# Decode kernel: other cuts of the loads, 1728 floats of kept V in three PSUM banks, 3840 floats of the first W_q held, first MLP in 22 loads

## The chip, the core and the metric

The kernel runs on one core of a Trainium2 chip. TensorE (PE) multiplies, VectorE (DVE) and ScalarE (ACT) work on rows, SyncE (SP) issues nearly all loads. The loads are carried by 16 DMA engines from HBM into SBUF. The metric is the device time of one execution in microseconds (us); three runs were taken of the kernel before.

## The reference

One token for each of four sequences goes through attention and a gated MLP, twice, with the same weights and caches in both layers. Only the last 1024 of 4096 cached positions are used. All data are float32.

```python
x = A_x                                            # 4 x 1 x 640
x = x + _A_ref(_layernorm(x), k_cache, v_cache, wq, wo)
x = x + _B_ref(_layernorm(x), W_gate, W_up, W_down)
x = x + _A_ref(_layernorm(x), k_cache, v_cache, wq, wo)
x = x + _B_ref(_layernorm(x), W_gate, W_up, W_down)
# _A_ref: q = x @ wq (32 heads of 128); softmax(q k^T / sqrt(128)) v over 1024 positions; then @ wo
# _B_ref: h = relu(x @ W_gate) * (x @ W_up), 1728 wide; h @ W_down
```

## The kernel before

Everything the kernel multiplies by lies in HBM as three matrices of 128 rows: `heads` (W_q, K, V, W_o of 27 heads, in the order of use), `kept` (the same of the last five heads, 27 to 31) and `mlp` (25,920 columns: the products of the last 192 hidden units first, then three gates of 5120 columns, then W_down in blocks of 640). A column is one float32 in each of 128 partitions, 512 bytes; sizes below are in columns, which the code and the title call floats.

In SBUF there is one large tile `store` of 51,840 columns, and `first_q` with the first 3072 columns of `heads`, which stay for both layers. At the end of layer 0's attention the 47,360 columns of `kept` lie at the start of `store` (`FRONT` is their end) and are used again at the start of layer 1, without a second load. All else is loaded twice.

The list of loads, `plan`, is written out by hand in the order in which SP issues them: layer, matrix, first and last column, place in `store`. `live` marks the columns of `store` that are still in use. After each product, `done` marks its operand's columns free, and `load` issues loads from the list for as long as the next one's place is free. SP then waits for the product that frees the place. So the order of issue is fixed, and a load can hold up those behind it.

Groups of heads are worked on in turn: the scores of the next group (line 396, PE), its softmax (line 407, ACT), then the values of this group (line 427, PE) and the projection of the one before (line 461). Layer 0 runs groups 0 to 8, with the kept groups 7 and 8 last (`K0`, `K1`); layer 1 begins with these two.

Between the two attentions stands the first MLP. Its weights don't fit beside `kept`, so they go through a ring of six places: three of 1280 columns behind `FRONT`, the last 640 columns of `store`, and two places taken from `kept`. `AHEAD` is 768 columns of the kept W_q; line 484 copies them into `probs`. `BACK` is 1280 columns of the kept V of head 29; line 485 copies 1024 of them into the two PSUM banks of `ps`, and line 435 copies 256 into the right part of `po`. In layer 1, when the K below `HOME` has been used, lines 400 and 401 copy the V from PSUM into `store` at `HOME`. `get` finds the place of an operand: in `first_q`, in `probs`, at `HOME`, or in the load that has it. It wants the whole operand in one place, so loads end where products end. Two products are cut in two by hand, at `CUT` (line 363) and at the start of `BACK` (line 426).

In `forward`, `gate(3)` uses the first 1920 columns, `gate(0)` to `gate(2)` 5120 each in products of 256 columns (line 519, four at a time on four parts of the array), and `down` W_down in blocks of 640 as four products of 160 (line 550), with a filler product (line 298) behind each block in layer 0.

The ring of the first MLP and the loads behind it:

```python
slots = [FRONT, FRONT + 1280, FRONT + 2560, BACK[0], AHEAD[0], STORE - D]
for i, n in enumerate([1280] * 4 + [768, 512] + [(768, 512), 1280, 1280, 1280, 768, 512]
                      + [1280, 1280, 1280, WD0 + D + 2 * QUARTER - 17280, D, D] + [1280] * 4 + [D, D]):
```

Of the kernel before, what the change touches and what calls it, by code (L numbers as in the profile page):

```python
# [59 lines left out]
HELD = 3072  # L60
STORE = 51840
# [4 lines left out]
BACK = FRONT - 2 * KV - 1280, FRONT - 2 * KV  # L66
HOME = 12672
# [22 lines left out]
CUT = 1792  # L90
ROWS["heads"][2].append(len(HEADS[0]) * D + CUT)
ROWS["heads"][2].sort()
ROWS["mlp"] = {}, MLP, [*range(0, GU0, P), *range(GU0, WD0, 256), WD0, TAIL, *range(WD1, MLP + 1, D)]
# [5 lines left out]
def decode_kernel(ctx: ExitStack, tc: tile.TileContext, x, source, sel, out):  # L99
# [20 lines left out]
    def put(layer, row, to, *cuts):  # L120

        for lo, hi in zip(cuts, cuts[1:]):
            assert hi - lo <= MOST and to % 64 == 0 and lo in known[row] and hi in known[row], (row, lo, hi)
            assert to + hi - lo <= STORE, (row, lo, hi, to)
            plan.append((layer, row, lo, hi, to))
            to += hi - lo
        return to
# [18 lines left out]
    known = {row: set(cuts) for row, (_, _, cuts) in ROWS.items()}  # L146
# [23 lines left out]
    assert lo == MLP  # L170


    k, cut = at_part("k", 0), at_part("q", 1) + CUT
# [7 lines left out]
    lo, to = lo + 8704, HOME + BACK[1] - BACK[0]  # L181
    for n in 4608, 6144, 9728:
        hi = near(lo + n)
        to = put(1, "heads", to, lo, hi)
        lo = hi
# [34 lines left out]
    def get(layer, row, lo, n):  # L220
        if row == "heads" and lo + n <= HELD:
            return first_q[:, lo:lo + n]
        if row == "kept" and layer and AHEAD[0] <= lo < AHEAD[1]:
            return probs[:, QUARTER + lo - AHEAD[0]:][:, :n]
        if row == "kept" and layer and BACK[0] <= lo < BACK[1]:
            return store[:, HOME + lo - BACK[0]:][:, :n]
        for first, m, p in held[key(layer, row)]:
            if first <= lo and lo + n <= first + m:
                return store[:, p + lo - first:p + lo - first + n]
        raise KeyError((layer, row, lo, n))  # L230
# [18 lines left out]
    def part(layer, what, h, lo, n):  # L249

        row, first = WHERE[what, h]
        return get(layer, row, first + lo, n)
# [26 lines left out]
    nc.vector.memset(pp, 0.0)  # L279
# [8 lines left out]
    y = ps_y.tile([P, QUARTER], F32, name="y")  # L288
# [68 lines left out]
    def query(layer, g, spread=False):  # L357


        n = len(HEADS[g]) * P  # L360
        qp[g] = ps_m.tile([P, n], F32, tag="m", name="qp")
        for c in range(KC - 1):
            for a, b in [(0, CUT - c * n), (CUT - c * n, n)] if g == 1 and c * n < CUT < c * n + n else [(0, n)]:
                nc.tensor.matmul(qp[g][32 * c:32 * c + 32, a:b], xT[:, B * c:B * c + 32],  # L364
                                 part(layer, "q", g, c * n + a, b - a),
                                 start=True, stop=c > 0 and not spread or b < n, tile_position=(0, 32 * c))
        part_done(layer, "q", g, 0, (KC - 1) * n)
        c = KC - 1
        m = n // 4 if spread else n
        for a in range(n // m):  # L370
            nc.tensor.matmul(qp[g][32 * a:32 * a + 32, a * m:a * m + m], xT[:, B * c:B * c + 32],  # L371
                             part(layer, "q", g, c * n + a * m, m), start=False, stop=True, tile_position=(0, 32 * a))
        part_done(layer, "q", g, c * n, n)
# [14 lines left out]
    def scores(layer, g):  # L388
        n = len(HEADS[g])
        to = sc[g] = pp if layer and g == order[1][0] else ps  # L390
        for i, h in enumerate(HEADS[g]):
            for j in range(2):
                for b in range(B):
                    lo = (j * B + b) * 512
                    at = SIDE - 1 + SIDE * (B * i + b) - i
                    nc.tensor.matmul(to[32 * b:32 * b + SIDE, j, :], qT[:, at:at + SIDE], part(layer, "k", h, lo, 512),  # L396
                                     start=i == 0, stop=i == n - 1, tile_position=(0, 32 * b))
                    part_done(layer, "k", h, lo, 512)
                    if to is pp and k0 + i * KV + lo < HOME + BACK[1] - BACK[0] <= k0 + i * KV + lo + 512:
                        nc.scalar.copy(store[:, HOME:HOME + 1024], ps.rearrange("p j n -> p (j n)"))  # L400
                        nc.scalar.copy(store[:, HOME + 1024:HOME + 1280], po[:, P:3 * P])
        nm[g] = small.tile([P, 1], F32, name="nm")
        nc.vector.tensor_reduce(nm[g], to.rearrange("p j n -> p (j n)"), axis=AX.X, op=ALU.max, negate=True)  # L403
# [9 lines left out]
    def values(layer, g, last=False):  # L413


        n = len(HEADS[g])
        for i, h in enumerate(HEADS[g]):
            t = pT[i % 2]
            to = t[:, GAP:].rearrange("p (c x) -> p c x", c=8)[:, :, :B]
            for j in range(2):  # L420
                nc.vector.tensor_copy(to[:, 4 * j:4 * j + 4], pp[:, j].rearrange("p (c x) -> p c x", c=4)[:, :, i:P:32])  # L421
            for c in range(8):
                a = c % 4
                at = GAP + SIDE * B * c - B * i
                cut = BACK[0] - at_part("v", h) - c * 512
                for x, z in [(0, cut), (cut, 512)] if g >= K0 and 0 < cut < 512 else [(0, 512)]:
                    nc.tensor.matmul(po[32 * a:32 * a + SIDE * B, x:z], t[:, at:at + SIDE * B],  # L427
                                     part(layer, "v", h, c * 512 + x, z - x),
                                     start=i == 0 and c < 4, stop=i == n - 1 and c >= 4 and z == 512, tile_position=(0, 32 * a))
                part_done(layer, "v", h, c * 512, 512)  # L430
        if last:
            nc.vector.tensor_copy(gates[:, 2 * P:], po[:, 2 * P:])  # L432
            nc.scalar.copy(gates[:, :2 * P], po[:, :2 * P])
            if layer == 0:
                nc.scalar.copy(po[:, P:3 * P], store[:, BACK[1] - 256:BACK[1]])
                free(*BACK)
        else:
            nc.scalar.copy(gates, po)  # L438
# [18 lines left out]
    def project(layer, g, last=False):  # L457
        o = oT.pop(g)
        for i, h in enumerate(HEADS[g]):
            for a in range(4):  # L460
                nc.tensor.matmul(y[32 * a:32 * a + B], o[:, i], part(layer, "o", h, a * QUARTER, QUARTER),  # L461
                                 start=False, stop=last and h == HEADS[g][-1], tile_position=(0, 32 * a))
            part_done(layer, "o", h, 0, D)

    def attention(layer):
# [14 lines left out]
        for before, g, after, then in zip([None] + gs, gs, gs[1:] + [None], gs[2:] + [None] * 2):  # L480
            totals(g)
            turned()
            if layer == 0 and after is None:
                nc.scalar.copy(probs[:, QUARTER:QUARTER + 768], store[:, AHEAD[0]:AHEAD[1]])
                nc.scalar.copy(ps.rearrange("p j n -> p (j n)"), store[:, BACK[0]:BACK[0] + 1024])
                free(*AHEAD)
# [21 lines left out]
    def forward(layer):  # L508
# [3 lines left out]
        def gate(j):  # L512
# [3 lines left out]
            for c in range(KC):  # L516
                for g in range(groups):
                    lo = at + (c * groups + g) * 2 * n
                    nc.tensor.matmul(gus[j][32 * g:32 * g + 32, :2 * n], xT[:, B * c:B * c + 32], get(layer, "mlp", lo, 2 * n),  # L519
                                     start=c == 0, stop=c == KC - 1, tile_position=(0, 32 * g))  # L520
# [24 lines left out]
        def down(j, last=False):  # L545
            for f in range(4 if j < 3 else 1):
                lo = WD1 + j * WD + f * D if j < 3 else WD0
                w = get(layer, "mlp", lo, D)
                for g in range(4):
                    nc.tensor.matmul(y[32 * g:32 * g + B], hTs[j][:, f], w[:, g * QUARTER:(g + 1) * QUARTER],  # L550
                                     start=False, stop=last and f == 3, tile_position=(0, 32 * g))
# [5 lines left out]
            if j == 3:  # L557
                w = get(layer, "mlp", TAIL, 2 * QUARTER)
                for g in range(4):
                    r = slice(64 * (g // 2), 64 * (g // 2) + 64)  # L560
                    nc.tensor.matmul(y[32 * g:32 * g + B], hTs[j][r, 1], w[r, g % 2 * QUARTER:(g % 2 + 1) * QUARTER],
                                     start=False, stop=False, tile_position=(r.start, 32 * g))
# [83 lines left out]
```

## Time and profile before

| | |
|---|---|
| median of three runs | 733.49 us (733.29 to 733.76) |
| profiled execution | 733.02 us |
| its span, first to last instruction | 731.2 us |
| read from HBM | 311.19 MB, 426 GB/s over the span |
| mean granted TensorE clock | 0.818 |
| loads issued by SP: `heads`, `kept`, `mlp` | 46 with that of `first_q`, 10, 34 |

A row of the windows view has, for one stretch of the span, the busy time of each engine and its number of instructions, the granted clock, the mean busy share of the 16 DMA engines and the rate. A row of the landing times has the time from a load's issue to the semaphore that says it is in. A row of the chain of waits has start, length and what ran or was waited for. A timeline row has start, length, engine, line, operation, tiles and count, and in brackets the idle time before it with what ended it. One product in float32 is two matmul records in the trace.

### The profile page before, as it was taken

How to read it: one execution, taken by the hardware profiler on the slowest of the kernel's cores; microseconds unless marked ns; L12 is line 12 of the kernel's file. 1: busy time of each engine (PE TensorE's matmuls, PEld its weight loads, DVE VectorE, ACT ScalarE, POOL GpSimd, SP SyncE). 2: the span in 40 equal slices, each digit the busy share in tenths (PEclk: the TensorE clock that was granted, in tenths of full speed). 3: DMA queues.
4: the chain of work that ended last, by engine and by line, in shares of the span. 5: the costliest groups of instructions: out<-in, count | busy, mean ns of one | idle time of the engine just before them, and what ended most of it. 6: DMA issues, size and time to landing. Idle time of an engine off the chain costs nothing.

```text
span 731.2 us, 8241 instructions
## 1 busy us (share of the span) xinstructions
PE 440.8 (60%) x3755; PEld 140.9 (19%) x3755; DVE 76.1 (10%) x280; ACT 50.5 (7%) x93; POOL 0.2 (0%) x4
## 2 busy tenths in 40 slices
PE   0846565655555555519778995465656556555576
PEld 0211111111111111103333231021111012111233
DVE  1111000010010101002101221001011010101011
ACT  0200000000000000000301210000000000000100
POOL 0000000000000000000000000000000000000000
PEclk9978787877777787759999999677778677877999
DMA  9999999999999999999999999999999999999996
GB/s 414 400 445 438 445 438 405 439 444 438 422 430 438 422 443 442 422 428 421 421 401 410 437 426 452 427 445 425 442 438 411 445 440 444 410 435 432 428 425 286
DMA packets 13290, 311.80 MB, mean 426 GB/s; under 512 B 1476, under 2 KB 1732, under 8 KB 6984
## 3 DMA queue, kind: packets, MB, share of 16 engines
q1 hardware_dynamic: 13104, 311.19, 99.1%
q8 instruction: 29, 0.48, 0.2%
q10 hardware_dynamic: 152, 0.09, 0.0%
q14 instruction: 5, 0.04, 0.0%
HBM read 311.19 MB, written 0.08 MB: 426 GB/s over the span
## 4 chain that ended last, share of the span: by engine, by line
DMA 75%; PE 23%; DVE 1%; issue 1%; ACT 0%; SPq 0%; ACTq 0%; DVEq 0%
DMA store<-in_heads 56%; PE ps L396 9%; DMA store<-in_kept 9%; DMA store<-in_mlp 7%; PE po L427 5%; DMA sel_sb<-in_sel 3%; PE qp L364 1%; PE pp L411 1%; PE y L461 1%; PE qp L371 1%; PE pp L396 1%; PE pp L519 1%; PE qt L383 1%; PE ot L451 0%; PE y L550 0%
## 5 line engine op out<-in xcount | busy, mean ns | idle before, releaser
L396 PE MATMUL ps<-store,qT 128*4 128x512 f32 x976 | 154.1, 711 | 119.9 <-DMA store<-in_heads 97.9
L427 PE MATMUL po<-store,pT 128*16 128x512 f32 (+1 forms) x1028 | 151.9, 708 | 122.4 <-DMA store<-in_heads 116.5
L427 PEld LDWEIGHTS po<-store,pT 128*16 128x16 f32 x1028 | 32.5, 109 | 226.9 <-issue 118.5
L396 PEld LDWEIGHTS ps<-store,qT 128*4 128x4 f32 x976 | 28.4, 95 | 227.3 <-DMA store<-in_heads 110.0
L403 DVE TENSOR_REDUCE nm<-ps 128x1 f32<-128x1024 f32 x17 | 20.8, 1225 | 255.4 <-PE ps L396 255.4
L407 ACT ACTIVATE probs<-ps,nm 128x1024 f32<-128x1024 f32 x17 | 18.9, 1113 | 328.8 <-DVE nm L403 328.8
L421 DVE COPY pT<-pp 128x16 f32<-128x16 f32 x128 | 17.1, 169 | 135.1 <-PE po L427 135.1
L461 PE MATMUL y<-store,oT 128*4 128x160 f32 x512 | 23.6, 317 | 10.6 <-DMA store<-in_heads 9.0
L438 ACT COPY gates<-po 128x512 f32<-128x512 f32 x16 | 9.4, 586 | 247.6 <-PE po L427 247.6
L519 PE MATMUL pp<-store,xT 128*32 128x256 f32 (+1 forms) x300 | 21.8, 363 | 6.7 <-DVE gates L529 3.1
L411 PE MATMUL pp<-sel_sb,probs 128*128 128x128 f32 x144 | 20.8, 293 | 0.0
L411 PEld LDWEIGHTS pp<-sel_sb,probs 128*128 128x128 f32 x144 | 18.7, 155 | 0.0
L364 PE MATMUL qp<-store,xT 128*32 128x512 f32 (+2 forms) x124 | 18.5, 586 | 0.0
L444 DVE RECIPROCAL r<-so 128x16 f32<-128x16 f32 x18 | 4.6, 257 | 131.2 <-PE so L442 131.2
L461 PEld LDWEIGHTS y<-store,oT 128*4 128x4 f32 x512 | 12.8, 90 | 19.6 <-DMA store<-in_heads 9.4
L371 PE MATMUL qp<-store,xT 128*32 128x512 f32 (+3 forms) x38 | 15.1, 505 | 0.0
L376 DVE TENSOR_SCALAR gates<-qp,rstd 128x512 f32<-128x512 f32 (+2 forms) x18 | 12.4, 690 | 17.5 <-PE qp L371 16.0
L291 PE MATMUL y<-probs,sel_sb 4*4 4x160 f32 x8 | 0.7, 444 | 21.2 <-DMA sel_sb<-in_sel 21.2
L519 PEld LDWEIGHTS pp<-store,xT 128*32 128x32 f32 x300 | 10.0, 109 | 16.3 <-DMA store<-in_mlp 7.1
L550 PE MATMUL y<-store,hT 128*4 128x160 f32 x208 | 10.3, 299 | 3.5 <-DMA store<-in_mlp 3.4
L383 PE MATMUL qt<-sel_sb,gates 128*128 128x128 f32 x64 | 12.3, 315 | 0.0
L451 PE MATMUL ot<-sel_sb,gates 128*128 128x128 f32 x72 | 11.3, 277 | 1.2 <-DVE gates L432 1.2
(79 smaller groups left out, 133.2 us busy)
## 6 DMA issues: line engine op xcount, KB each, us to landing
store<-in_heads SPq DMA_DIRECT2D x20, 7936.0 KB, 45.2
store<-in_heads SPq DMA_DIRECT2D x3, 8128.0 KB, 36.0
store<-in_mlp SPq DMA_DIRECT2D x15, 640.0 KB, 6.6
store<-in_kept SPq DMA_DIRECT2D x2, 4096.0 KB, 40.7
store<-in_heads SPq DMA_DIRECT2D x1, 8000.0 KB, 43.7
store<-in_heads SPq DMA_DIRECT2D x1, 7744.0 KB, 46.0
store<-in_heads SPq DMA_DIRECT2D x1, 7552.0 KB, 35.8
store<-in_heads SPq DMA_DIRECT2D x1, 7424.0 KB, 34.6
```

Of the source, the lines that this page charges most:

```text
L364: nc.tensor.matmul(qp[g][32 * c:32 * c + 32, a:b], xT[:, B * c:B * c + 32], part(layer, "q", g, c * n + a, b - a), start=True, stop=c > 0 ...
L371: nc.tensor.matmul(qp[g][32 * a:32 * a + 32, a * m:a * m + m], xT[:, B * c:B * c + 32], part(layer, "q", g, c * n + a * m, m), start=False ...
L376: nc.vector.tensor_scalar(gates[:, :len(HEADS[g]) * P], qp.pop(g), rstd, SCALE, op0=ALU.mult, op1=ALU.mult)
L383: nc.tensor.transpose(qt[:, i], gates[:, i * P:(i + 1) * P], ident)
L396: nc.tensor.matmul(to[32 * b:32 * b + SIDE, j, :], qT[:, at:at + SIDE], part(layer, "k", h, lo, 512), start=i == 0, stop=i == n - 1, tile_ ...
L403: nc.vector.tensor_reduce(nm[g], to.rearrange("p j n -> p (j n)"), axis=AX.X, op=ALU.max, negate=True)
L407: nc.scalar.activation(probs, sc.pop(g).rearrange("p j n -> p (j n)"), AF.Exp, bias=nm.pop(g), accum_out=sums[g])
L411: nc.tensor.transpose(pp[:, c // 4, c % 4 * P:c % 4 * P + P], probs[:, c * P:(c + 1) * P], ident)
L421: nc.vector.tensor_copy(to[:, 4 * j:4 * j + 4], pp[:, j].rearrange("p (c x) -> p c x", c=4)[:, :, i:P:32])
L427: nc.tensor.matmul(po[32 * a:32 * a + SIDE * B, x:z], t[:, at:at + SIDE * B], part(layer, "v", h, c * 512 + x, z - x), start=i == 0 and c ...
L461: nc.tensor.matmul(y[32 * a:32 * a + B], o[:, i], part(layer, "o", h, a * QUARTER, QUARTER), start=False, stop=last and h == HEADS[g][-1], ...
L519: nc.tensor.matmul(gus[j][32 * g:32 * g + 32, :2 * n], xT[:, B * c:B * c + 32], get(layer, "mlp", lo, 2 * n), start=c == 0, stop=c == KC - ...
```

## The change

- `first_q` holds 3840 columns and `store` has 51,072, so layer 1's loads of `heads` begin at column 3840.
- `BACK` is 1728 columns. 1024 of them rest in `ps`, 384 in `po` and 320 in the bank of `y`, whose tile `yy` is now 512 columns wide with the accumulator `y` in its first 160. `HOME` moves with it.
- The first MLP goes through five places of 1280, 1792, 768, 1728 and 640 columns in the same order throughout, 22 loads in all with one of 640 first and one of 448 last; before, 26.
- The first loads of layer 1 are 2624, 768, 1728, 640 and 448 columns into these places, from column 3840 on in order, then 1216, 1024, 1024, 2048 and 3584 into the place of the kept W_q and K.
- `get` is replaced by `place` and `product`: an operand that lies in two loads is multiplied in two pieces. Loads may end at any multiple of 64 columns.
- The memset of `pp` at the start is gone.

```diff
-HELD = 3072
-STORE = 51840
+HELD = 3840
+STORE = 51072
-BACK = FRONT - 2 * KV - 1280, FRONT - 2 * KV
-HOME = 12672
+BACK = FRONT - 2 * KV - 1728, FRONT - 2 * KV
+HOME = 12864
...
-    slots = [FRONT, FRONT + 1280, FRONT + 2560, BACK[0], AHEAD[0], STORE - D]
     lo = put(0, "mlp", STORE - D, 0, D) - STORE + D
-    for i, n in enumerate([1280] * 4 + [768, 512] + [(768, 512), 1280, 1280, 1280, 768, 512]
-                          + [1280, 1280, 1280, WD0 + D + 2 * QUARTER - 17280, D, D] + [1280] * 4 + [D, D]):
-        for m in n if type(n) is tuple else [n]:
-            put(0, "mlp", slots[i % 6] if m == n or m == 768 else FRONT + 768, lo, lo + m)
-            lo += m
+    slots = [(FRONT, 1280), (FRONT + 1280, STORE - D - FRONT - 1280), (AHEAD[0], 768), (BACK[0], 1728), (STORE - D, D)]
+    for i in range(21):
+        at, n = slots[i % 5]
+        end = min(lo + n, MLP)
+        put(0, "mlp", at, lo, end)
+        lo = end
+    rest = (MLP - D) % (STORE - FRONT + 768 + 1728)
...
-    to = put(1, "heads", FRONT, k, k + 1536, k + 2560, k + 3584)
-    put(1, "heads", BACK[0], HELD, cut)
-    put(1, "heads", AHEAD[0], cut, k)
-    put(1, "heads", to, k + 3584, k + 4096)
-    lo = k + 4096
-    to = put(1, "heads", AHEAD[1], lo, lo + 1024, lo + 2048, lo + 3072, lo + 5120, lo + 8704)
+    lo = HELD
+    for at, n in (FRONT + rest, STORE - D - FRONT - rest), *slots[2:], (FRONT, rest):
+        put(1, "heads", at, lo, lo + n)
+        lo += n
+    to = AHEAD[1]
+    for n in 1216, 1024, 1024, 2048, 3584:
+        to = put(1, "heads", to, lo, lo + n)
+        lo += n
-    for n in 4608, 6144, 9728:
+    for n in 4096, 6144, 9728:
...
+    def place(layer, row, lo):
+        if row == "heads" and lo < HELD:
+            return first_q, lo, HELD - lo
+        most = KV
+        if row == "kept" and layer:
+            if AHEAD[0] <= lo < AHEAD[1]:
+                return probs, QUARTER + lo - AHEAD[0], AHEAD[1] - lo
+            if BACK[0] <= lo < BACK[1]:
+                return store, HOME + lo - BACK[0], BACK[1] - lo
+            most = min(x - lo for x in (AHEAD[0], BACK[0], FRONT) if x > lo)
+        for first, m, p in held[key(layer, row)]:
+            if first <= lo < first + m:
+                return store, p + lo - first, min(first + m - lo, most)
+
+    def product(out, by, layer, row, lo, n, start, stop, rows=slice(0, P), **how):
+        a = 0
+        while a < n:
+            t, p, m = place(layer, row, lo + a)
+            z = min(n, a + m)
+            nc.tensor.matmul(out[:, a:z], by, t[rows, p:p + z - a], start=start and not a, stop=stop and z == n, **how)
+            a = z
...
-    y = ps_y.tile([P, QUARTER], F32, name="y")
+    yy = ps_y.tile([P, 512], F32, name="y")
+    y = yy[:, :QUARTER]
...
-                        nc.scalar.copy(store[:, HOME + 1024:HOME + 1280], po[:, P:3 * P])
+                        nc.scalar.copy(store[:, HOME + 1024:HOME + 1408], po[:, P:])
+                        nc.scalar.copy(store[:, HOME + 1408:HOME + 1728], yy[:, QUARTER:3 * QUARTER])
...
-                nc.scalar.copy(po[:, P:3 * P], store[:, BACK[1] - 256:BACK[1]])
+                nc.scalar.copy(po[:, P:], store[:, BACK[0] + 1024:BACK[0] + 1408])
...
                 nc.scalar.copy(ps.rearrange("p j n -> p (j n)"), store[:, BACK[0]:BACK[0] + 1024])
+                nc.scalar.copy(yy[:, QUARTER:3 * QUARTER], store[:, BACK[1] - 320:BACK[1]])
```

More of the change, by code (lines that the diff above doesn't have):

```diff
@@ L218, in key @@
         return (0 if row == "kept" else layer), row
[L220 to L226, printed above, removed]
-        for first, m, p in held[key(layer, row)]:
-            if first <= lo and lo + n <= first + m:
-                return store[:, p + lo - first:p + lo - first + n]
-        raise KeyError((layer, row, lo, n))
+    def place(layer, row, lo):
[8 more added lines that the diff above has]
+            most = min(x - lo for x in (AHEAD[0], BACK[0], FRONT) if x > lo)
+        for first, m, p in held[key(layer, row)]:
+            if first <= lo < first + m:
+                return store, p + lo - first, min(first + m - lo, most)
+        raise KeyError((layer, row, lo))
+    def product(out, by, layer, row, lo, n, start, stop, rows=slice(0, P), **how):
[5 more added lines that the diff above has]
+            a = z
     def done(layer, row, lo, n):
@@ L251, in part @@
         row, first = WHERE[what, h]
-        return get(layer, row, first + lo, n)
+        return layer, row, first + lo, n
     def part_done(layer, what, h, lo, n):
@@ L362, in query @@
         for c in range(KC - 1):
[L363 to L366, printed above, removed]
+            product(qp[g][32 * c:32 * c + 32], xT[:, B * c:B * c + 32], *part(layer, "q", g, c * n, n),
+                    start=True, stop=c > 0 and not spread, tile_position=(0, 32 * c))
         part_done(layer, "q", g, 0, (KC - 1) * n)
@@ L424, in values @@
                 at = GAP + SIDE * B * c - B * i
[L425 to L429, printed above, removed]
+                product(po[32 * a:32 * a + SIDE * B], t[:, at:at + SIDE * B], *part(layer, "v", h, c * 512, 512),
+                        start=i == 0 and c < 4, stop=i == n - 1 and c >= 4, tile_position=(0, 32 * a))
                 part_done(layer, "v", h, c * 512, 512)
@@ L460, in project @@
             for a in range(4):
-                nc.tensor.matmul(y[32 * a:32 * a + B], o[:, i], part(layer, "o", h, a * QUARTER, QUARTER),
-                                 start=False, stop=last and h == HEADS[g][-1], tile_position=(0, 32 * a))
+                product(y[32 * a:32 * a + B], o[:, i], *part(layer, "o", h, a * QUARTER, QUARTER),
+                        start=False, stop=last and h == HEADS[g][-1], tile_position=(0, 32 * a))
             part_done(layer, "o", h, 0, D)
@@ L547, in down @@
                 lo = WD1 + j * WD + f * D if j < 3 else WD0
[L548 removed]
                 for g in range(4):
[L550 to L551 removed]
+                    product(y[32 * g:32 * g + B], hTs[j][:, f], layer, "mlp", lo + g * QUARTER, QUARTER,
+                            start=False, stop=last and f == 3, tile_position=(0, 32 * g))
                 done(layer, "mlp", lo, D)
```

31 lines of the change are left out of this document (11 added, 20 removed).

## The prediction

> **What bounds the kernel now.** I read the page first (busy shares, transfer rows, chain), then the windows view over stages, then landing times of the loads that SP issues, and last TensorE's timeline in the first MLP.
>
> ```profile
> span 731.2 us, 8241 instructions
> PE 440.8 (60%) x3755; PEld 140.9 (19%) x3755; DVE 76.1 (10%) x280; ACT 50.5 (7%) x93; POOL 0.2 (0%) x4
> DMA  9999999999999999999999999999999999999996
> q1 hardware_dynamic: 13104, 311.19, 99.1%
> q8 instruction: 29, 0.48, 0.2%
> DMA 75%; PE 23%; DVE 1%; issue 1%; ACT 0%; SPq 0%; ACTq 0%; DVEq 0%
> ```
>
> The DMA engines are busy in every slice but the last; the loads alone fill 99.1% of 16 engines' span. The chain names PE for 23%, but those are stretches in which PE was working while transfers ran as well: it can follow one path only. So the time is bytes over rate, plus what the engines idle.
>
> ```profile
> 480.00:690.00 210.00, 124.20 (x935) 36.99 (x937) 18.88 (x75) 11.02 (x18) 0.00 (x0) 0.77 1.00 434
> 371.00:373.00 2.00, 1.97 (x20) 0.56 (x18) 0.00 (x0) 0.00 (x0) 0.00 (x0) 1.00 0.96 316
> 373.00:395.00 22.00, 17.50 (x201) 7.18 (x203) 1.58 (x7) 1.10 (x3) 0.00 (x0) 1.00 1.03 415
> 363.00:395.00 32.00, 25.84 (x334) 11.75 (x328) 2.89 (x13) 2.39 (x8) 0.00 (x0) 1.00 1.02 406
> 395.00:450.00 55.00, 52.50 (x506) 18.13 (x501) 12.93 (x40) 9.75 (x18) 0.00 (x0) 1.00 1.02 434
> 690.00:727.00 37.00, 26.05 (x392) 11.89 (x388) 4.10 (x17) 2.77 (x9) 0.00 (x0) 0.95 0.93 398
> ```
>
> Columns: stretch, length, busy time of PE, PEld, DVE, ACT, POOL, granted clock, DMA share, GB/s. Large loads run at 434 GB/s. The first MLP (363 to 395) gets 406: its 26 loads are small, and between 371 and 373 the rate falls to 316 with a share of 0.96, the one place in the middle of the run where the engines run short. The last 37 us show something else:
>
> ```profile
> 696.96 30.70 DMA store<-in_mlp
> ```
>
> This link of the chain is the last load: issued at 696.96, landed 30.7 us later, so from 697 on the queue holds all that is left, and still the share of 690 to 727 is 0.93. The 16 engines don't finish together; the end waits for the latest of them.
>
> ```profile
> DMA to landing us min/median/max: 13.5/43.8/62.4
> DMA to landing us min/median/max: 5.1/5.6/8.9
> DMA to landing us min/median/max: 5.6/6.7/7.3
> DMA to landing us min/median/max: 30.7/39.6/49.1
> out_x<-probs SPq DMA_DIRECT2D x1, 80.0 KB, 1.6
> ```
>
> The first four rows are the loads of line 211, by issue: 0 to 340, 363 to 372, 372 to 391, 447 to 690. Loads of the heads wait behind 30 us of queue and more (13.5 is the least, ahead of the first MLP); nothing a few microseconds long can empty that. In the first MLP a load lands 5 to 7 us after its issue, and a 640 KB load moves in 1.5 us (655,360 B at 434 GB/s), so 4 to 5 us is queue and start. The last row is a transfer into an empty queue: 1.6 us, 0.2 of it for its bytes, so a load needs at most 1.4 us from issue to landing beside its bytes. A load issued with less than that queued ahead can leave engines idle.
>
> **The change, part by part.**
>
> *768 more floats of W_q stay.* Layer 1 starts its reload at column 3840 and not 3072: 768 x 512 B = 393,216 B less, 0.91 us at 434 GB/s (0.92 at the mean 426). Layer 0 moves the same bytes. As transfers fill the span, all of it is on the path: **-0.91**. The first load is longer by as much, but the loads behind it take 43.8 us to land at the median, so nothing early in layer 0 reaches the end.
>
> *22 loads for 26 in the first MLP.* The other counts stay: 27 in layer 0 ahead of it, 29 and 8 in layer 1. What a small load costs beside its bytes: from 373 to 395 the rate is 415, so 22 x (1 - 415/434) = 0.96 us is lost, over 9.13 MB or some 17 loads: 0.057 each. With the short spot, 32 x (1 - 406/434) = 2.06 us over 26 loads: 0.08 each. Four fewer are worth 0 to 0.32 us; I take 0.057 each: **-0.23**. The Trainium skill, in DMA: Bandwidth & Descriptors (Anatomy of one DMA), fits a transfer as about 2.0 us fixed plus bytes at 436 GB/s, measured on the gpsimd path. By it four loads would be worth 8 us; the trace agrees for a load alone (1.4 us at most) and disagrees for queued ones (0.06 us).
>
> *A smaller ring.* The slots of the first MLP were six with 6528 floats and become five with 6208 (1280, 1792, 768, 1728, 640): 7.3 us of transfers for 7.7. Two places count. At 371 PE has just begun to hand slots back, since the layernorm stands ahead:
>
> ```profile
> 366.72 1.11 PE pp L519 x25
> 369.33 1.51 PE pp L519 x20
> 370.86 6.27 DMA store<-in_mlp
> ```
>
> Before, 8320 floats were issued when the slot behind the second load was asked for; now 8128 are, by the same products (seven of gate(0) for five, both in its second group of four). That is 192 floats, 0.23 us shallower at a spot already short: 0 to 0.23 us lost, taken 0.1.
>
> The other is new. The first load of layer 1 (2624 floats) covers the last of two slots, and so waits until columns up to 22336 are used. That is the middle of W_down's block 22080 to 22720, so also for the next load and for four blocks of PE work after the 1792 load lands:
>
> ```profile
> 390.23 0.46 PE L550 MATMUL y<-store,hT 128*4 128x160 f32 x8
> 390.62 0.33 PE L298 MATMUL po<-sel_sb 128*128 128x128 f32 x1
> 390.78 0.27 PE L536 MATMUL ph<-sel_sb,gates 128*128 128x128 f32 x1
> 391.11 0.46 PE L550 MATMUL y<-store,hT 128*4 128x160 f32 x8
> 391.75 0.46 PE L550 MATMUL y<-store,hT 128*4 128x160 f32 x8
> 392.63 0.46 PE L550 MATMUL y<-store,hT 128*4 128x160 f32 x8 [0.17 <-DMA store<-in_mlp]
> ```
>
> A block with its filler takes 0.64 us (391.11 to 391.75), the turn of the hidden row adds 0.24. So 3 x 0.64 + 0.24 + 0.46 = 2.6 us, with SP's step some 2.8. Queued behind the 1792 load are 768 + 1728 + 640 + 448 = 3584 floats, 1.84 MB, 4.2 us. About 1.4 us are left (1.1 if the semaphore comes 0.3 late), against a start of at most 1.4. So 0 to 0.4 us is lost on the latest engine; taken 0.1. The earlier engines may idle a microsecond, but they wait at the end anyway. Together: **+0.2**, between 0 and 0.63. The skill's same page (Why a DMA increments its semaphore by 16) says that a load counts as landed only when every engine used has added its one; no run here shows the count. By it idle time of an early engine is free, as I take it; were all 16 in step, both spots would cost in full.
>
> Other laps are deeper: a slot comes back when the load behind its own has landed, with at worst 1280 + 1792 floats off the queue; 3136 floats (3.7 us) stay, less about 1 us of PE work. Behind the MLP, loads into the kept W_q's place follow.
>
> ```profile
> 395.62 0.73 PE y L550 x16
> 399.76 0.41 PE qp L371 x2
> ```
>
> The last blocks of W_down start at 395.62, their load just in, and the kept W_q is used at 399.8 but for its last piece: 4.2 us, in which 6208 floats (7.3 us) are queued; before, 6144 were. Some 3 us remain, no less than before.
>
> *Split products.* Before, 4 products are cut in two; after, 23: 2 in q, 5 in the first k, 1 in v, 15 in the first MLP. Nineteen more pieces at 0.06 to 0.2 us (a whole product of four in L550's row takes 0.115) are 1 to 4 us of PE, 0.9 to 3 of it in the first MLP, where PE idles 32 - 25.84 = 6.2 us. From 395 to 450 PE has 2.5 us idle, but the queue grows there and the rate is 434. Zero, unless a piece stands ahead of a release (then 0.1, within the bounds above).
>
> *Copies.* ScalarE gains two copies of 320 columns, and two of 256 become 384.
>
> ```profile
> L485 ACT COPY ps<-store 128x1024 f32<-128x1024 f32 x1 | 1.0, 1011 | 0.0
> L435 ACT COPY po<-store 128x256 f32<-128x256 f32 x1 | 0.4, 377 | 0.0
> 405.55 0.38 ACT L401 COPY store<-po 128x256 f32<-128x256 f32 x1
> 407.67 1.11 ACT L407 ACTIVATE probs<-pp,nm 128x1024 f32<-128x1024 f32 x1 [1.74 <-DVE nm L403]
> ```
>
> ```profile
> 357.26 0.20 ACT L349 ACTIVATE t<-eps_sb 128x1 f32<-128x1 f32 x1
> 361.70 0.37 ACT L433 COPY gates<-po 128x256 f32<-128x256 f32 x1 [4.24 <-DVE gates L432]
> 362.50 1.00 PE L461 MATMUL y<-store,oT 128*4 128x160 f32 x24
> 431.43 0.86 PE L461 MATMUL y<-store,oT 128*4 128x160 f32 x20
> ```
>
> (1011 - 377)/768 = 0.83 ns a column: 0.43 us for 320, 0.1 for 128 more. In layer 0 the 0.43 falls ahead of a gap of 4.24 us on ScalarE; the load into BACK waits for L435 and slips 0.1, with 4480 floats (5.3 us) ahead of it in the queue. In layer 1 the copies end 0.53 later, in a gap of 1.74 ahead of the exponential. Zero. Nor does sharing y's bank bind: y's next products stand at 362.50, six microseconds after the copy in, and at 431.43, 25 after the copy out. Dropping one memset in the start: zero.
>
> **The sum**: 0.91 + 0.23 - 0.2 = 0.94 us less. The profiled execution took 733.02 us (span 731.2, 1.8 around it): 732.1 by it. It lies 0.47 below the median of 733.49, the lowest of the three runs being 733.29; from the median the same difference gives 732.55, and I say **732.5**. That is 0.13%; a measurement tells 0.2% (1.5 us) from no change.
>
> **Rivals.**
>
> *A. The ring runs dry and eats the gain.* For it: the 316 GB/s at 371, where 2 x (1 - 316/434) = 0.54 us went missing with a deeper ring. Two such spots cost 1.1 and leave nothing: 733.2 to 734.2. Against: the share there is only 0.06 below its neighbours, 0.12 us of 16 engines; most of them had work. Chance 0.17.
>
> *B. Slower: each lap runs dry.* One mechanism: a slot comes back only when PE has used a block that needs the next load too. It costs as soon as that lag passes the queue left, 3.7 us less the start of 1.4, so from 2.3 us of PE lag. At 0.54 us a spot, five of them give +2.7 - 1.1 = +1.6: 735.1; six, 735.6. Against, from TensorE's timeline:
>
> ```profile
> 375.64 1.05 PE L519 MATMUL pp<-store,xT 128*32 128x256 f32 x10 [0.59 <-DMA store<-in_mlp]
> 377.18 1.05 PE L519 MATMUL pp<-store,xT 128*32 128x256 f32 x10 [0.49 <-DMA store<-in_mlp]
> ```
>
> The products of a 1280 load take 1.05 us, and the next load comes 1.54 us after the last: PE waits for loads, and its lag stays near one. Chance 0.08.
>
> *C. The lateness of single engines shifts.* 8241 instructions make 29 fetches, 284 each; 76 more (19 pieces in two passes, each with its weights) are 0.27 of one. A fetch is 16.5 KB on one engine, 0.6 us at 27 GB/s. If fetches fall on other engines, or the spot at 371 goes, the end moves by 0.5 to 1: 731.0 to 731.9 on the fast side. Chance 0.14.
>
> *D. The fixed price of a load is real*, as the fit has it: four loads at 1.4 us by the rows are 5.6, so 727; by the page 8, so 725. Speaks against: 99.1% busy leaves no such time. Chance 0.01.
>
> **How the numbers follow.** The bounds give 0.91 + 0.32 = 1.23 less and 0.91 - 0.63 = 0.28 less, so the forecast spans 732.2 to 733.2, with a chance of 0.60. With A and half of C, and 0.25 for the spread of the runs, 731.6 to 734.2 holds 0.8. Faster by over 0.2% (below 732.0): C, D and 0.07 of the forecast, whose lower end lies 0.2 from that line: 0.22. Slower (above 735.0): B, 0.08. The rest, 0.70.
>
> **What would show it.** q1 at 310.8 MB; 86 loads; share 1.0 and 406 to 415 GB/s in the first MLP; landings there of 4 us and more, and the 2624-float load's close to its bytes plus 2 to 3; the last landing of in_mlp about 0.9 us earlier. Wrong, if a window near 394 falls below 350 GB/s and the end is no earlier, or if PE, not a load, leads the chain in the last 200 us.

## The result and the profile after

| | kernel before | changed kernel |
|---|---|---|
| median of four runs | 733.44 us | 740.96 us (739.6 to 741.73) |
| ratio, 95% interval | | 1.010 (1.0082 to 1.0118) |
| profiled execution, span | 733.02, 731.2 us | 741.69, 739.5 us |
| read from HBM | 311.19 MB | 310.80 MB |

Slower by 7.5 us, where 0.9 us less was forecast. The page of the changed kernel, its span, the transfer rows by slice and the load queue:

```profile
span 739.5 us, 8312 instructions
DMA  9999999999999999998998999999999999999997
GB/s 391 440 440 437 440 437 400 445 435 433 438 439 430 425 441 426 433 414 353 420 382 301 422 447 440 431 430 440 437 434 436 420 444 419 436 437 424 426 430 292
q1 hardware_dynamic: 12528, 310.79, 98.2%
```

The saved bytes are there. But the share of the span that loads fill is 98.2% for 99.1%, and the slices that begin at 333 and at 388 us have 353 and 301 GB/s. The windows view of the changed kernel shows both:

```profile
334.00:337.00 3.00, 3.00 (x50) 1.30 (x54) 1.82 (x7) 1.20 (x2) 0.00 (x0) 1.00 0.65 186
373.00:395.00 22.00, 12.25 (x155) 5.25 (x143) 1.35 (x6) 1.10 (x3) 0.00 (x0) 0.94 1.00 373
395.00:400.00 5.00, 5.00 (x54) 2.48 (x54) 0.00 (x0) 0.00 (x0) 0.00 (x0) 0.56 0.64 219
400.00:410.00 10.00, 9.66 (x153) 4.97 (x148) 2.24 (x8) 2.47 (x6) 0.00 (x0) 1.00 0.87 327
480.00:690.00 210.00, 120.80 (x878) 34.40 (x878) 17.91 (x68) 8.95 (x15) 0.00 (x0) 0.77 1.00 432
```

The kernel before, in the stretches not yet shown:

```profile
334.00:337.00 3.00, 3.00 (x51) 1.31 (x51) 1.80 (x7) 1.20 (x2) 0.00 (x0) 1.00 0.94 404
395.00:400.00 5.00, 4.70 (x80) 2.35 (x75) 1.57 (x5) 2.42 (x6) 0.00 (x0) 1.00 1.01 408
400.00:410.00 10.00, 9.39 (x75) 3.40 (x74) 2.97 (x7) 2.54 (x5) 0.00 (x0) 1.00 1.04 425
```

The last two columns are DMA share and GB/s, the third from the end the granted clock. Large loads run as fast as before (432 for 434). The time went in two places: 334 to 337 us, still in layer 0's attention, and the first MLP with what follows it.

*First place.* SP's waits from 299 to 338 us, in the kernel before and then in the changed one (engine, line, for whom: total, times, longest):

```profile
SPq L211 <- PE po L427: 25.2, 1, 25.2
SPq L211 <- DMA store<-in_heads: 9.6, 1, 9.6
SPq L211 <- PE so L442: 3.3, 1, 3.3
```

```profile
SPq L207 <- PE y L238: 36.2, 1, 36.2
SPq L207 <- PE po L238: 2.1, 1, 2.1
```

SP stands still for most of this time in both kernels; what differs is the load that it stands at. Before, the load of kept V (8192 columns, 9.7 us of transfers) to 26,880 to 35,072 was issued at 301.7 us, and SP then stood at the load behind it until 336.8. In the changed kernel SP stands at this load itself, 36.2 us for a projection, and issues it at 335.0, when the load ahead of it is almost in (335.8), so the queue runs empty. Layer 0's last three loads of `heads` fill the store up to its end, so the column where they begin is the end of `heads` less the room: with 768 columns less in `store`, rounded up to the end of a product, they begin 1024 columns later in the matrix. Everything in them then lies 1024 columns lower in the store, W_o of group 5 at 34,048 instead of 35,072. Before, the load of kept V ended just where that W_o began. Now it needs 1024 columns of it, and they are used only after the scores of group 7, at 335 us.

*Second place.* The chain of waits of the changed kernel (start, length, what):

```profile
365.61 9.01 DMA store<-in_mlp
...
375.78 7.26 DMA store<-in_mlp
383.08 1.06 PE pp L238 x12
...
385.63 7.15 DMA store<-in_mlp
392.82 1.07 PE pp L238 x3
```

These are three loads into one place, `BACK`, of 1728 columns. One is issued at 365.61, the next at 375.78, the next at 385.63: ten microseconds for a lap of the ring that holds 6208 columns, or 7.3 us of transfers. Of a lap, 7.2 us pass from issue to landing, and 2.55 from the first product on the load (383.08) until the place is handed on (385.63): its last 256 columns belong to the first product of gate(2), which stands behind the turn from one gate to the next. TensorE's waits for loads from 369 to 402 us, in the kernel before and in the changed one:

```profile
PE pp L519 <- DMA store<-in_mlp: 2.7, 6, 0.6
PE y L550 <- DMA store<-in_mlp: 1.0, 3, 0.6
```

```profile
PE pp L238 <- DMA store<-in_mlp: 9.1, 6, 3.4
```

TensorE waited up to 0.6 us for a load and now waits up to 3.4. Behind the longest wait its granted clock falls to half (0.56 in the window 395 to 400), just as W_down is due and its blocks must free places for layer 1.

### The profile page after: what moved, and what is told of

It reads as the page before. It is cut to its first block, busy times and chain, and to the rows that moved or that the text cites. A ratio compares the mean times of both kernels' runs of the same rounds, so it can differ in the third digit from the quotient of the medians.

```text
span 739.5 us, 8312 instructions
## 1 busy us (share of the span) xinstructions
PE 443.2 (60%) x3795; PEld 142.6 (19%) x3795; DVE 75.1 (10%) x279; ACT 51.4 (7%) x95; POOL 0.2 (0%) x4
## 3 DMA queue, kind: packets, MB, share of 16 engines
q1 hardware_dynamic: 12528, 310.79, 98.2%
HBM read 310.80 MB, written 0.08 MB: 420 GB/s over the span
## 4 chain that ended last, share of the span: by engine, by line
DMA 76%; PE 23%; DVE 1%; issue 0%; ACT 0%; SPq 0%; DVEq 0%; ACTq 0%
DMA store<-in_heads 60%; PE ps L238 10%; DMA store<-in_kept 9%; DMA store<-in_mlp 7%; PE po L238 5%; PE y L238 2%; PE qp L238 1%; PE pp L238 1%; PE pp L418 1%; PE qt L389 1%; PE po L306 0%; PE ot L455 0%; PE so L446 0%; DVE nm L410 0%; ACT probs L414 0%
## 5 line engine op out<-in xcount | busy, mean ns | idle before, releaser
L238 PE MATMUL po<-store,pT 128*16 128x512 f32 (+1 forms) x1026 | 154.6, 715 | 125.1 <-DMA store<-in_heads 116.3
L238 PE MATMUL ps<-store,qT 128*4 128x512 f32 (+2 forms) x986 | 153.2, 703 | 113.1 <-DMA store<-in_heads 91.2
L238 PE MATMUL qp<-store,xT 128*32 128x512 f32 (+3 forms) x154 | 29.0, 579 | 7.5 <-DMA store<-in_heads 7.5
L238 PE MATMUL pp<-store,xT 128*32 128x256 f32 (+3 forms) x318 | 20.4, 354 | 12.9 <-DMA store<-in_mlp 9.1
L238 PE MATMUL y<-store,hT 128*4 128x160 f32 (+3 forms) x238 | 12.3, 316 | 1.8 <-DMA store<-in_mlp 1.8
L389 PEld LDWEIGHTS qt<-sel_sb,gates 128*128 128x128 f32 x64 | 7.5, 154 | 19.3 <-issue 16.4
```

Source lines behind the costliest of these rows:

```text
L238: nc.tensor.matmul(out[:, a:z], by, t[rows, p:p + z - a], start=start and not a, stop=stop and z == n, **how)
L389: nc.tensor.transpose(qt[:, i], gates[:, i * P:(i + 1) * P], ident)
```

## The experiments

Times are medians; "before" is the kernel before, run on the same chip beside them, 733.3 to 733.5 us throughout.

### The late load

The changed kernel with the load cut at W_o's new place:

```diff
-put(0, "kept", k0, k0, k1, v0, v0 + 2 * KV, v1, ...)
+put(0, "kept", k0, k0, k1, v0, v0 + 7168, v0 + 2 * KV, v1, ...)
```

> The changed kernel, with the load of kept V into 26880 to 35072 cut at 34048, where W_o of group 5 still lies. Theory 1 (that load waits for the projection of group 5 and leaves the queue empty at 335 us): its first 7168 columns are issued near 302 us as in the kernel before, the idle stretch at 335 goes, and the time falls by 3.0 us, to 737.5 to 738.5. Rival (the time is lost in the first MLP only, by the cut products): no change beyond 0.5 us.

Measured: 736.46 us, 4.5 less than the changed kernel; 1.0043 of before (1.0029 to 1.0057). The windows view of e1_cut:

```profile
334.00:337.00 3.00, 3.00 (x50) 1.23 (x52) 1.72 (x7) 1.21 (x2) 0.00 (x0) 1.00 0.93 403
385.00:395.00 10.00, 7.58 (x91) 3.17 (x91) 0.67 (x3) 0.37 (x1) 0.00 (x0) 0.83 0.94 358
395.00:405.00 10.00, 9.65 (x141) 4.64 (x144) 2.21 (x7) 2.47 (x6) 0.00 (x0) 1.00 0.92 347
```

The kernel before in the last two of these stretches:

```profile
385.00:395.00 10.00, 8.94 (x118) 3.69 (x122) 0.67 (x3) 0.37 (x1) 0.00 (x0) 1.00 1.03 411
395.00:405.00 10.00, 9.67 (x125) 4.01 (x124) 2.21 (x7) 2.83 (x7) 0.00 (x0) 1.00 1.02 409
```

The idle stretch at 335 is gone (403 GB/s for 186); the first MLP stays slow. The gain was larger than the 3.0 expected. The same fault put into the kernel before:

```diff
-put(0, "kept", k0, k0, k1, v0, v0 + 2 * KV, v1, ...)
+put(0, "kept", k0, k0, k1, v0, v0 + 2 * KV + 1024, v1, ...)
```

> The kernel before, with the same load made 1024 columns longer, so that it reaches into the place of group 5's W_o. Theory 1: it is issued near 335 us instead of 301.7, the engines idle there for 2 to 3 us, and the time rises by 2.5 to 3.5 us, to 736 to 737. Rival: same time as before, since nothing else is changed.

Measured: 736.26 us, 2.8 more than before (1.0037, 1.0024 to 1.005). SP's waits from 299 to 336 us in e2_late, then its windows:

```profile
SPq L211 <- PE y L461: 36.7, 1, 36.7
```

```profile
334.00:337.00 3.00, 3.00 (x50) 1.33 (x54) 1.82 (x7) 1.21 (x2) 0.00 (x0) 1.00 0.71 218
385.00:395.00 10.00, 8.55 (x107) 3.38 (x99) 0.67 (x3) 0.37 (x1) 0.00 (x0) 1.00 1.02 418
```

One longer load makes the wait of the changed kernel and its idle stretch, with the first MLP left at its old rate. So the late load is a cause by itself and costs 2.8 us.

### The ring: first tries

e1_cut with fillers in the gates, against the half clock:

```diff
+                if j < 3:
+                    busy(2)
```

> e1_cut with two filler products behind each fifth part of the three large gates (both layers). Theory 2a (the ring is late because TensorE idles, and the granted clock then falls to 0.5 just as W_down is due): the clock stays at 1.00 through the first MLP, the first load of layer 1 is issued some 3 us earlier, and the time falls by 2 to 3 us against e1_cut, to 735 to 736. Theory 2b (the ring is late by its cuts, the clock only follows): the clock may stay up, but the time falls by less than 1 us.

Measured: 737.51 us, 1.0 more than e1_cut. The clock did stay at 1.00 (windows view of e3_fill), and the rate stayed low:

```profile
385.00:395.00 10.00, 8.57 (x108) 3.79 (x100) 0.61 (x3) 0.37 (x1) 0.00 (x0) 1.00 0.98 371
395.00:405.00 10.00, 8.66 (x130) 4.40 (x129) 1.76 (x7) 2.47 (x6) 0.00 (x0) 1.00 0.96 358
```

So the low clock is not what makes the ring late. What it costs isn't told, since the fillers themselves delay products.

e1_cut with one end put at the end of gate(1):

```diff
         end = min(lo + n, MLP)
+        if lo < GU0 + 2 * GU < end:
+            end = GU0 + 2 * GU
```

> e1_cut with one load of the ring ended at the end of gate(1) (column 12160, 1472 columns in place of 1728), so that its place no longer waits for the first product of gate(2). Theory 2b (a place is held over the turn from one gate to the next): the load behind it is issued 2 us earlier, the wait of 3.4 us for it on TensorE goes, with it the fall of the clock, and the time falls by 2 to 4 us against e1_cut. Theory 2a: the fall of the clock may move but stays, and the gain is under 1 us.

Measured: 735.5 us (734.86 to 738.29), 1.0 less than e1_cut. Its profiled execution took 737.63 us, the second longest of its ten; its windows view shows the clock falling earlier:

```profile
373.00:385.00 12.00, 7.64 (x76) 4.26 (x75) 0.86 (x4) 0.73 (x2) 0.00 (x0) 0.72 0.93 340
```

The rate of 340 GB/s is low as well. One end is part of it at most.

e1_cut with the first load of layer 1 in two, each in one place:

```diff
-        put(1, "heads", at, lo, lo + n)
+        put(1, "heads", at, lo, *([lo + 1280 - rest] if n == 3072 - rest else []), lo + n)
```

> e1_cut with the first load of layer 1 (2624 columns) in two, 832 and 1792, each at the end of its own place. The step of the prediction that put a loss of 0 to 0.4 us at this load: it is issued 2 to 3 us earlier, with 3 us queued instead of 1.4. If the dry spot near 396 us is its doing, the time falls by 0.5 to 1.5 us against e1_cut; if the ring was already late, by less than 0.4.

Measured: 736.06 us, 0.4 less than e1_cut, inside the scatter of either. The prediction's spot is small, if it costs anything; the ring was late before it.

### The ring: ends, places, depth

e1_cut with 28 loads that end with products and gates, in places of up to 1536 columns (list in short):

```diff
+    for at, n in [(F0, 1280), (F1, 1280), (F2, 512), (BB, 1536), (AA, 768), (S, 512), (F0, 512),
+                  (F0 + 512, 768), (F1, 1280), (F2, 512), (BB, 1536), (AA, 768), (S, 256),
...
```

> e1_cut with the first MLP in 28 loads that all end where products and gates end, in the same 6208 columns (at most 6016 of them in use, places of 1280, 1280, 512, 1536, 768, 640). Theory E (ends inside products and across the turn of a gate hold the places): TensorE's waits of 1.5 to 2.4 us for single loads go, and the time falls by 2 to 3.5 us against e1_cut, to 733 to 734.5. Theory D: as shallow as the ring of the change or more, so no gain, 736 or more.

Measured: 736.02 us (734.59 to 740.04). No gain. But at most 6016 columns of its ring are in use, 192 fewer than in e1_cut, so this run doesn't tell the ends from the depth.

The old layout with all ends moved by 128 columns:

```diff
-enumerate([1280] * 4 + [768, 512] + ... + [1280] * 4 + [D, D])
+enumerate([1152] + [1280] * 3 + [768, 512] + ... + [1280] * 4 + [D + 128, D])
```

> The layout and ring of the kernel before (3072 of W_q, 1280 of V, six places, 6528 columns, 26 loads), in the changed kernel's code, with every end in the first MLP moved down by 128 columns, into the middle of a product and across the turns of the gates. Theory E: the time rises by 1 to 3 us over the kernel before, to 734.5 to 736.5. Theories D and G: the places are as many and as large as before, so 733.5 to 734.2. That the code of the pieces itself costs something would show here too.

Measured: 734.97 us (733.45 to 737.12), 1.6 more than before (1.002, 1.0007 to 1.0033). Ends inside products and across the turns of the gates cost something even in the old ring, unless it is the code of the pieces; e5_seven, next, has that code and loses nothing by it.

The 6208 columns of the change as seven places, ends inside products as in the change:

```diff
-    slots = [(FRONT, 1280), (FRONT + 1280, STORE - D - FRONT - 1280), (AHEAD[0], 768), (BACK[0], 1728), (STORE - D, D)]
+    slots = [(FRONT, 1024), (FRONT + 1024, 1024), (FRONT + 2048, 1024), (AHEAD[0], 768), (BACK[0], 832),
+             (BACK[0] + 832, 896), (STORE - D, D)]
```

> e1_cut with the ring's 6208 columns as seven places (three of 1024, then 768, 832, 896, 640) in 30 loads, ends still inside products. Theory G (the places are too coarse: a 1728 place is held until its last column and the load behind it are in, so a lap of the ring takes 8.2 us where its bytes take 7.4): each place comes back sooner, the rate in the first MLP rises, and the time falls by 1.5 to 3 us against e1_cut (736.5), to 733.5 to 735, though eight loads more cost 0.5. Theory D (the ring is too shallow, 6208 for 6528): within 0.7 us of e1_cut or slower.

Measured: 732.9 us, 3.6 less than e1_cut. Its windows, and then TensorE's waits for loads from 369 to 402 us, first of e1_cut, then of e5_seven:

```profile
385.00:395.00 10.00, 9.49 (x132) 4.26 (x124) 0.67 (x3) 0.37 (x1) 0.00 (x0) 1.00 1.03 413
395.00:405.00 10.00, 9.65 (x127) 4.15 (x130) 2.21 (x7) 2.64 (x7) 0.00 (x0) 1.00 1.04 416
```

```profile
PE pp L238 <- DMA store<-in_mlp: 6.9, 5, 2.4
```

```profile
PE pp L243 <- DMA store<-in_mlp: 4.0, 9, 0.7
```

With eight loads more in the first MLP, the rate is back at 413 and 416 GB/s, the longest wait is 0.7 us, and the clock stays up. The profiled execution of the same kernel in e11_again (below) did have half the clock for 3.4 us:

```profile
381.10:384.50 3.40, 3.25 (x33) 1.64 (x37) 0.00 (x0) 0.00 (x0) 0.00 (x0) 0.50 1.03 414
```

The rate stayed at 414 GB/s, and it took 732.91 us: a fall of the clock alone doesn't make the ring late. The same from the other side, two places of the kernel before in one:

```diff
-slots = [FRONT, FRONT + 1280, FRONT + 2560, ...]      # 1280 each
+F0, F1 = FRONT, FRONT + 1280                          # 1280 and 2560
```

> The kernel before with two of its six places taken as one of 2560 columns: same 6528 columns, same ends (all at the ends of products), four loads fewer. Theory G (coarse places empty the queue, since a place comes back only when all of it is used): TensorE waits for the 2560 load in each lap, the rate in the first MLP falls below 390 GB/s, and the time rises by 2 to 5 us, to 735.5 to 738.5. Rival (what counts is depth, or that ends lie inside products): 733.2 to 733.8, or 0.2 less for the loads saved.

Measured: 737.72 us, 4.4 more than before (1.0056, 1.0043 to 1.0069), with old depth, old ends and four loads fewer. Its windows and waits for loads from 369 to 402 us:

```profile
395.00:405.00 10.00, 9.68 (x119) 3.95 (x112) 1.61 (x5) 2.47 (x6) 0.00 (x0) 0.74 0.92 325
```

```profile
PE pp L519 <- DMA store<-in_mlp: 4.5, 3, 2.1
PE y L550 <- DMA store<-in_mlp: 2.7, 1, 2.7
```

Two waits of 2.1 us and one of 2.7 are for loads of 2560; the third in the first row is 0.3 us, for a small load. Which place of the change it is: one of the two large ones split at a time, `(FRONT + 1280, 896), (FRONT + 2176, 896)` in e14_back, `(BACK[0], 832), (BACK[0] + 832, 896)` in e15_front.

> e1_cut with the 1792 place in two of 896 and the 1728 place whole (six places). If the 1728 place, reissued only once gate(2) has begun, is the one that holds the ring up: 735.5 or more, TensorE still waiting 1.5 to 2.5 us for it in each lap. If the largest place is what counts: 734 to 735.5.

> e1_cut with the 1728 place in two (832 and 896) and the 1792 place whole (six places). If the 1728 place holds the ring up: 733 to 734.3, near e5_seven. If coarse places count alike: about as e14_back, 734 to 735.5.

Measured: 735.63 us (734.53 to 738.36) with `BACK` whole, 733.86 (733.29 to 737.65) with `BACK` split. Splitting the 1792 place brings 0.8 of e5_seven's 3.6, which is inside the scatter; splitting the 1728 place brings 2.6.

e5_seven with 320 columns of the ring empty:

```diff
-    slots = [(FRONT, 1024), (FRONT + 1024, 1024), (FRONT + 2048, 1024), ...]
+    slots = [(FRONT, 960), (FRONT + 960, 960), (FRONT + 1920, 832), ...]
```

> e5_seven with 320 columns of the ring left empty (5888 in seven places of 640 to 960). Theory G with fine places: the queue is still long enough when a place comes back, and the time stays within 0.7 us of e5_seven, 732.5 to 733.5. Theory D (depth decides): the step from 6208 to 5888 is as large as the one from 6528 to 6208, and the time rises by 1.5 us or more.

Measured: 734.72 us, with runs from 732.49 to 737.35. My expectation of 733.5 at most failed: depth counts as well, and at 5888 columns the ring holds in some executions and not in others.

### What is left of the gain

e5_seven again, with more runs.

> e5_seven once more, with more rounds beside the kernel before. If the 0.9 us of transfers that the change saves are on the path once the two stalls are mended, less 0.6 for nine loads more than in the kernel with the mended kept load: 0.2 to 0.8 us below the kernel before, 732.6 to 733.2. If something else in the change costs as much, no difference.

Measured: 732.76 us against 733.32, 0.6 less (0.9994, 0.9984 to 1.0003). The direction is as reckoned, 0.91 for the bytes less 0.46 for eight loads more than the kernel before; the interval includes no change. (For e5_seven the ratio was 0.9999, 0.9989 to 1.0008.)

320 columns more of W_q, and the kept load cut anew:

```diff
-HELD, STORE = 3840, 51072
+HELD, STORE = 4160, 50752
-put(0, "kept", k0, k0, k1, v0, v0 + 7168, v0 + 2 * KV, v1, ...)
+put(0, "kept", k0, k0, k1, v0, v0 + 6656, v0 + 2 * KV, v1, ...)
```

> e10_shallow with the 320 freed columns given to W_q (4160 held, 50752 in the store) and the load of kept V cut where W_o of group 5 now begins. If bytes are on the path and the ring of fine places holds: 0.38 us below e10_shallow, some 0.5 to 1.2 below the kernel before, 732.2 to 732.9. If another load is caught by the moved layout, an idle stretch shows in layer 0 and the time is 733.5 or more.

Measured: 734.41 us (732.62 to 736.53), 0.3 less than e10_shallow, where its bytes give 0.38, but far inside the scatter of both. The expected 732.2 to 732.9 was missed: the time is above before, as e10_shallow's is. No idle stretch shows in layer 0.

The late load with the fine ring:

> The changed kernel with the ring of seven places of e5_seven, its load of kept V uncut. If the two stalls add up: e5_seven's time and the 2.8 us that the late load alone cost in e2_late, 735.3 to 736.3, so that the further 1.7 us which the cut brought on the coarse ring belong to the ring. If the late load costs the 4.5 us that its cut brought, 737 to 737.8.

Measured: 735.49 us, 2.7 more than e11_again. So the late load by itself is worth 2.7 to 2.8, with the ring of the kernel before and with that of seven places. With the coarse ring the losses don't simply add up: 2.7 and 3.6 make 6.3, and the changed kernel lies 8.2 above e11_again. The remaining 1.9 us arise only where both meet; how was not tested.

## Why the prediction was wrong

*What bounds.* Right: bytes over rate, plus idle transfers. Both losses are idle transfers, and with both mended the time comes out where the bytes put it, as far as an interval of 0.9984 to 1.0003 can tell.

*768 floats of W_q stay, "nothing early in layer 0 reaches the end".* This step failed, by 2.8 us. I counted layer 0's bytes and loads, found both the same, and looked for no more; I didn't follow where a smaller `store` puts each load of layer 0 and what must be used before it. A depth of 43.8 us at the median says nothing of a load that waits 36.

*22 loads for 26: -0.23.* The unit price is not contradicted: e11_again, with eight loads more than before, keeps 0.56 of the 0.91, so 0.35 over eight, 0.04 each where I had 0.057. But its interval includes no gain at all, so no run shows the price. The Trainium skill's fit in DMA: Bandwidth & Descriptors (2.0 us fixed, Anatomy of one DMA) would have made those eight cost 16 us; e11_again disagrees, for queued loads. A lone transfer, at most 1.4 us here, is below that fit too.

*"Other laps are deeper ... 3.7 us stay, less about 1 us of PE work", against a start of 1.4.* This is the step that failed most, in two of its terms. The lag was sized at 1 us; it is 2.55 us for `BACK` (383.08 to 385.63), since a place that reaches over the turn of a gate waits for relu, product and transpose as well. And a start of 1.4 us, read from a lone transfer, is no measure of the queue that is needed. At 385.63 the load ahead of `BACK`'s still has 3.1 us to go until it lands (388.71), and yet `BACK`'s lands 4.07 us behind it, where its bytes take 2.0. The changed kernel meanwhile:

```profile
386.50:392.50 6.00, 1.57 (x24) 0.65 (x24) 0.00 (x0) 0.00 (x0) 0.00 (x0) 1.00 0.99 345
```

The load's first packet starts at 386.68, its last at 392.20: so some engines had run short while others were still behind, and the landing tells of the latest only. The other traces agree. Take each load issued between 373 and 400 us, and the time from its issue until the load ahead lands (where the trace has that landing). In the profiled executions of before, e2_late, e5_seven, e10_shallow, e11_again, e12_more and e13_nocut it is never under 3.7 us. In all others it falls to 3.3 or less: 1.5 in the changed kernel, 1.9 in e1_cut, 2.6 in e9_coarse. This time was not varied by itself. e14_back and e15_front show the 1728 place to be the larger part, e5_seven and e9_coarse that the size of places decides at the same depth. The coarse ring costs 3.6 us (e1_cut to e5_seven) and 5.5 when the late load stands ahead (the changed kernel to e13_nocut).

*"Idle time of an early engine is free".* Not borne out, though not tested alone. In a steady stretch a packet takes its bytes at 27.2 GB/s and 9 ns (6912 B in 0.262 us). Counted in the trace's records of single packets from 364 to 405 us:

```text
packets over 0.15 us longer than their bytes at 27.2 GB/s and 9 ns, and their excess in all
before 33, 13 us    e1_cut 95, 36 us    e5_seven 40, 12 us
```

They come in groups, right behind a load issued to a short queue (in e1_cut 20 of them between 392.1 and 393.6, behind the load issued at 391.15). In e1_cut only 3 packets were under way at 392.1 us, for 16 in the kernel before. So an engine that ran dry starts again with packets up to 0.9 us too long, and they count as busy. In the changed kernel from 373 to 395 such packets hold 28 us of excess, 0.08 of the 16 engines' time. That is why it shows a share of 1.00 there with 373 GB/s, and why I read the 0.96 at 371 us as nearly nothing.

*The spot at the first load of layer 1.* Placed right; its size (0 to 0.4) is not contradicted (e8_halves 0.4, inside the scatter), and it is not what mattered.

*Split products, copies, y's bank: zero.* Right as far as the runs tell. ScalarE in the changed kernel's timeline:

```profile
358.26 0.42 ACT L490 COPY y<-store 128x320 f32<-128x320 f32 x1
414.78 0.45 ACT L408 COPY store<-y 128x320 f32<-128x320 f32 x1
416.53 1.11 ACT L414 ACTIVATE probs<-pp,nm 128x1024 f32<-128x1024 f32 x1 [1.31 <-DVE nm L410]
```

The copies take about the 0.43 us reckoned and end ahead of the wait for the maximum; e5_seven has them and its split products as well, and comes out below the kernel before.

*Rivals.* B, "each lap runs dry", had the mechanism in part, with a chance of 0.08: places come back too late, and the mark I named, under 350 GB/s near 394, came (219 from 395 to 400). But `BACK`, the larger part, waited for the turn of the gate and not for the next load. I set B's price by TensorE's 1.05 us for a load's products in the middle of a gate, where the lag is least.

## What to carry to other kernels

Where a buffer changes size, list for every later load what lies in its place and when that is used; the same bytes in the same number of loads can still wait on another product. For a ring that a queue refills, reckon at each place: depth, less the place, less the load that must land behind it, less the longest lag until the place is free, turns between stages included; what is left must exceed the start of a lone transfer by some microseconds: here the rings that kept the rate had at least 3.7 us until the landing ahead, the others 3.3 or less at some load. Small places cost too little to measure here (0.35 us by the medians for eight loads more), and large ones cost 3.6 us.

## What was not expected of the hardware

A transfer engine that has run dry shows busy while it starts again, with packets of up to 0.9 us beside their bytes (e1_cut, changed kernel); so the share of busy time can read 1.00 at 373 GB/s, and the rate is the better witness. TensorE's clock was granted at half for 6.8 us from the end of a wait of 3.4 us (changed kernel), for 3.4 us behind one of 2.4 us (e1_cut), and for 3.4 us in e11_again, where no wait for a load passed 0.6 us. The Trainium skill, in TensorE: Matmul & The Clock Gate (Part 1: The HAM clock gate), has the half rate follow about 3.4 us of idling; the first wait agrees, the second was shorter, and the third run has no such wait. The ten runs of e10_shallow lie 4.9 us apart, the 29 of the kernel before beside them 1.7 us (732.98 to 734.65); but beside e13_nocut one run of the kernel before took 736.04, so how much of the scatter is the ring's isn't shown. What the half clock itself costs in the changed kernel stays open.
